# Block-sparse attention and a gated convolution layer on one core: other dummy products and q transposes in the head, a last output block in halves, and a new instruction order

## The chip, the core and the metric

The kernel runs on one core of a Trainium2 chip. The core has a matrix engine (PE), whose weight loads the profile lists apart (PEld), a vector engine (DVE), a scalar engine for activations (ACT), GpSimd (POOL) and a sync engine (SP). Each has its own queue of instructions and takes them in the order in which they were written; they wait for one another by semaphores. PE writes only to PSUM, a small memory of eight banks, from which DVE or ACT copy to the main on-chip memory (SBUF). DMA engines move data between SBUF and the chip's main memory. The metric is the device time of one execution in microseconds, lower is better.

## What is computed

Attention over q, k and v of shape (4, 8, 768, 64) with a mask of 32 x 32 blocks, and behind it a feed-forward layer with a gate made by a convolution over three positions:

```python
scores = (1/8) * q @ k.T                 # per batch and head, 768 x 768
mask   = near blocks | first and last block row and column | 3 drawn blocks a row
attn   = softmax(where(mask, scores, -1e9)) @ v
x      = attn as (4, 768, 512)
h      = relu(x @ w_in)                  # (4, 768, 1024)
c      = conv_w[0]*h[s-1] + conv_w[1]*h[s] + conv_w[2]*h[s+1]
out    = (h * sigmoid(c)) @ w_out        # (4, 768, 512), float32
```

## The kernel before

The kernel first makes a list of operations (`op(...)`): each has a name, the engines on which it may run, a function that writes its instructions, and the buffers that it takes or uses. Then `put_down` writes them in the order of a long string, `ORDER`: two characters choose an operation, a letter (P, A, V, G, S) its engine where it has a choice, and one more character each buffer that it takes. So the string alone sets the order in each engine's queue, the engine of each copy, and the buffer.

**Attention.** The 32 heads are 16 pairs, four to a batch. A sequence of 768 is cut into two segments of 384 positions (the last into 256 and 128), and the work into 144 units, 18 to a segment of 384. A unit is eight blocks of 128 x 128 scores. It has two groups of score products (`s`, L762) into one of two PSUM tiles `st`, one exponential on ACT over 128 x 1024 (`exp`, L773) into a tile `pt`, and two groups of eight products with v (`av`, L795) into `av`. The mask is 24 extra rows of q and k (partitions 64 to 87), so the score product adds it. After a pair's last unit of a segment DVE takes the reciprocal of the sums (`rcp`, L712) and multiplies (`norm`, L714); the result `xtok` is transposed by a DMA or, in four segments, by PE (`x_tr`, L733), with a copy `x_cp`.

**Getting q and k ready.** q and k must lie with the 64 channels on partitions. For pairs 0 to 5 PE transposes them (`k_tr`, L467; `q_tr`, L505 or L535), and DVE or ACT copy from PSUM into the tiles `e` and `o` (`k_cp`, `q_cp`; every such copy has line L341 on DVE and L337 on ACT, the lines of the helper `dcopy`). For later pairs a DMA transposes, and two copies (`stg_cp`) follow. There are two ways to transpose a half of q. `q_head` turns 64 columns at a time, six products for a pair, each giving 64 partitions by 128, and needs two copies, one of two thirds of the columns and one of one third. `q_half` turns 128 columns at a time, so three products for a pair, with two column groups on top of each other in the result, and needs four copies (two of 64 x 256, two of 64 x 128). Before, `q_head` is called for pair 0 alone, once for each head; `q_half` for all others (L548 to L553).

**The start.** Pair 0 is loaded as float32 by SP and ACT queues (k, q, the drawn blocks, then v as SP's fourth large transfer) and cast on chip (`cast_k`, `cast_q`, `v_cp`); pairs 1 to 3 come through POOL's queue, which converts. The mask rows of q come from six small products (`w24`, L311), cast by `m_q` (L321 on ACT, L323 on DVE); those of k by `m_k`. PE runs dummy products on a tile of zeros (`warm` with 256 columns and `fill` with 128, L229 to L233); the first thirteen stand ahead of everything, the others where the order puts them.

**Feed-forward.** For a segment, `f1` (L888) multiplies with w_in into a PSUM tile `mix`, `relu` (L908 on ACT, L910 on DVE) writes `hE`. The gate is, for each pair of channel groups, three `mul` (L940), two `add` (L948), a `tanh` (L987), `g1` (L990) and `g2` (L995, writes `gT`); in the last segment PE does the convolution with diagonal weights (`conv`, L959). `out_block` multiplies 128 positions with w_out, eight products of 512 columns (`f2`, L822), copies out of PSUM (`ev`) and sends 128 x 512 by SP (`out`, L833). In the last segment the sums lie in the tiles `st` (`tail`), which the scores no longer need, and the copy is made in two halves. A batch has six output blocks, t = 0 to 5. At the very end these are left: t = 2 and 3, whose gates come from the last segment but one, and t = 4 and 5 of the last segment. Their f2 steps stand in the order so that t = 3, 5, 2 and 4 end in this sequence.

## Time and profile before

| | |
|---|---|
| median of 3 runs | 214.99 us (214.48, 214.99, 215.62) |
| the profiled execution | 214.71 us |
| its span, first to last instruction | 212.7 us |
| busy: PE, DVE, ACT, POOL | 204.0, 187.9, 193.3, 60.7 us |
| exponentials on ACT | 144 of 1.03 us, 140.4 us busy |
| first and last exponential start | 8.5 and 193.2 us |
| bytes read and written | 23.08 and 6.29 MB |

A row of the timeline has the start in us, the length, the engine, line, operation, the tiles written and read with their shapes, and the count of like instructions merged into it; in brackets the idle time of the engine ahead of it and what ended that. Products on PE overlap: a row's length is that of the pipeline, and the rate is seen in the distance of starts. A row by stretches has the window, its length, then the busy time and count of PE, PEld, DVE, ACT and POOL, the granted clock, the share of DMA and GB/s. A row of the groups has line, engine, operation, tiles, shapes, count, busy us and mean ns of one, then the idle time just ahead.

### The profile page before, as it was taken

To read this page: it belongs to the slowest core of one execution; us is meant where nothing else is said; L and a number is where in the kernel's file an instruction comes from. 1 tells how busy PE (TensorE), PEld (TensorE's weight loads), DVE (VectorE), ACT (ScalarE), POOL (GpSimd) and SP (SyncE) were. 2 spreads that over 40 slices of the span, in tenths; PEclk is the share of its full clock that TensorE was granted. 3 is DMA by queue.
4 is the path that set the end of the run, shared out by engine and by line. 5 is a ranking of instruction groups with operands and counts; after the bars stand their busy time and mean duration, and the time that the engine had idled before them with its cause. 6 is when DMAs were issued, how large, how long until landed. Compare 5 with 4: busy or idle time off the path is not lost.

```text
span 212.7 us, 6843 instructions
## 1 busy us (share of the span) xinstructions
PE 204.0 (96%) x2705; PEld 155.0 (73%) x2705; DVE 187.9 (88%) x595; ACT 193.3 (91%) x258; POOL 60.7 (29%) x117
## 2 busy tenths in 40 slices
PE   7999999999999999999999999999999999999992
PEld 4688877878767776677678867776668867787740
DVE  4779999999998997799999994999999967999970
ACT  6699999799999999999999998999999977998752
POOL 8794145620736143210406153910000000000000
PEclk9999999999999999999999999999999999999999
DMA  6999986799494999894759957996524040010405
GB/s 168 191 172 192 173 112 93 91 160 108 65 128 65 148 194 151 112 139 98 149 97 210 147 81 113 135 134 136 143 84 127 12 127 2 3 54 0 148 3 197
DMA packets 48935, 24.81 MB, mean 117 GB/s; under 512 B 35120, under 2 KB 45832, under 8 KB 48904
## 3 DMA queue, kind: packets, MB, share of 16 engines
q0 software_dynamic: 19728, 11.05, 43.6%
q1 hardware_dynamic: 28888, 13.05, 28.9%
q8 instruction: 21, 0.34, 0.7%
q10 hardware_dynamic: 288, 0.30, 0.4%
q14 instruction: 10, 0.08, 0.1%
HBM read 23.08 MB, written 6.29 MB: 138 GB/s over the span
## 4 chain that ended last, share of the span: by engine, by line
PE 73%; DVE 20%; ACT 2%; DMA 1%; issue 1%; DVEq 0%; ACTq 0%
PE st L762 23%; PE mix L822 18%; PE mix L888 16%; PE av L795 12%; DVE m L940 4%; DVE o L341 4%; DVE e L341 3%; DVE m L948 2%; PE st L822 2%; DVE diag L388 2%; DVE hE L910 2%; DVE xtok L714 2%; DMA o2s<-in_k_dram 1%; ACT pt L773 1%; DVE xT L341 1%
## 5 line engine op out<-in xcount | busy, mean ns | idle before, releaser
L773 ACT ACTIVATE pt<-st 128x1024 bf16<-128x1024 f32 x144 | 140.4, 1029 | 4.5 <-PE st L762 3.7
L795 PE MATMUL av<-vt,pt 128*128 128x65 bf16 x1152 | 59.9, 193 | 0.4 <-DVE xtok L714 0.4
L795 PEld LDWEIGHTS <-pt 128*128 128x128 bf16 x1152 | 52.2, 97 | 9.5 <-ACT pt L773 0.7
L888 PE MATMUL mix<-xT,winb 128*128 128x384 bf16 (+2 forms) x288 | 54.3, 308 | 1.2 <-DVE hE L910 0.8
L940 DVE TENSOR_SCALAR m<-hE,cw 128x382 bf16<-128x382 bf16 (+2 forms) x192 | 49.2, 318 | 0.3
L822 PE MATMUL mix<-woutb,gT 128*128 128x512 bf16 x176 | 47.1, 379 | 0.0
L762 PE MATMUL st<-o 88*128 88x128 bf16 (+1 forms) x240 | 45.1, 230 | 0.0
L762 PE MATMUL st<-o,e 88*128 88x128 bf16 (+1 forms) x228 | 44.0, 235 | 0.3 <-ACT pt L773 0.2
L762 PE MATMUL st<-e,o 88*128 88x128 bf16 (+1 forms) x224 | 43.5, 236 | 0.2
L762 PE MATMUL st<-e 88*128 88x128 bf16 (+1 forms) x208 | 42.3, 243 | 0.6 <-DVE e L341 0.3
L762 PEld LDWEIGHTS <-o 88*128 88x128 bf16 x464 | 35.5, 98 | 8.1 <-issue 0.6
L762 PEld LDWEIGHTS <-e 88*128 88x128 bf16 x436 | 33.6, 98 | 8.7 <-issue 1.7
L948 DVE TENSOR_TENSOR m<-m 128x764 bf16<-128x764 bf16 (+2 forms) x64 | 34.1, 536 | 0.7
L888 PEld LDWEIGHTS <-winb 128*128 128x128 bf16 x288 | 23.5, 97 | 8.7 <-issue 1.8
L987 ACT ACTIVATE m<-m 128x764 bf16<-128x764 bf16 (+2 forms) x32 | 26.2, 823 | 1.7 <-DVE m L948 1.4
L822 PEld LDWEIGHTS <-gT 128*128 128x128 bf16 x192 | 15.7, 97 | 11.8 <-DVE gT L995 1.7
L415 POOL COPY pace<-pt 1x1 bf16<-1x1 bf16 x24 | 8.2, 342 | 55.5 <-ACT pt L773 55.4
L908 ACT ACTIVATE hE<-mix 128x384 bf16<-128x384 f32 (+2 forms) x39 | 18.9, 498 | 1.0 <-PE mix L888 1.0
L995 DVE TENSOR_TENSOR gT<-m,hE 128x764 bf16<-128x764 bf16 (+3 forms) x36 | 18.0, 510 | 0.5
L714 DVE TENSOR_TENSOR xtok<-av,rcp 128x384 bf16<-128x384 f32 (+2 forms) x36 | 18.1, 506 | 0.4
L240 POOL DMA_DIRECT2D nat<-in_q_dram x23 | 16.8, 729 | 2.5 <-issue 2.1
L910 DVE TENSOR_SCALAR hE<-mix 128x384 bf16<-128x384 f32 x25 | 13.7, 553 | 3.1 <-PE mix L888 1.6
(92 smaller groups left out, 174.5 us busy)
## 6 DMA issues: line engine op xcount, KB each, us to landing
out_dram<-o2s SPq DMA_DIRECT2D x24, 256.0 KB, 2.8
nat<-in_k_dram POOLq DMA_DIRECT2D x15, 192.0 KB, 4.7
vn<-in_v_dram POOLq DMA_DIRECT2D x15, 192.0 KB, 5.1
nat<-in_q_dram POOLq DMA_DIRECT2D x6, 192.0 KB, 4.6
winb<-in_moe_w_in_dram POOLq DMA_DIRECT2D x2, 512.0 KB, 8.0
woutb<-in_moe_w_out_dram POOLq DMA_DIRECT2D x4, 256.0 KB, 7.4
nat<-in_q_dram POOLq DMA_DIRECT2D x9, 96.0 KB, 4.7
nq<-in_q_dram POOLq DMA_DIRECT2D x6, 96.0 KB, 3.9
```

The source lines that it names most:

```text
L714: nm = op("norm", {"DVE": t_dps(128 * C)}, lambda e: nc.vector.tensor_tensor(out=xtok_t[xk.index][:, 0:C].rearrange("p c h d -> p h c d"), ...
L762: nc.tensor.matmul(out=st[:, 128 * x:128 * (x + n_)], lhsT=QK[kc % 2][s][0:88, 1, hh, kc // 2, :], rhs=QK[par][s][0:88, 0, hh, idx:idx + n ...
L773: nc.scalar.activation(out=pt_t[ptb.index], in_=st_t[stb.index], func=AF.Exp, bias=0.0, scale=0.125)
L795: nc.tensor.matmul(out=o[:, off:off + 65], lhsT=pt_t[ptb.index][:, 128 * x:128 * x + 128], rhs=V_t[vslot_b[P].index][:, hh, kc, 0:65], sta ...
L822: nc.tensor.matmul(out=acc(), lhsT=gT_t[gb.index][:, ffc, 128 * t:128 * t + 128], rhs=woutb[:, ffc, :], start=(ffc == 0), stop=(ffc == NFF ...
L888: nc.tensor.matmul(out=mix_t[hb.index][:, w1 * y:w1 * y + w1], lhsT=winb[:, fc, 128 * ffc:128 * ffc + 128], rhs=xT_t[xt_buf[n].index][:, f ...
L908: nc.scalar.activation(out=dst, in_=src, func=AF.Relu, bias=0.0, scale=0.5)
L910: nc.vector.tensor_scalar(out=dst, in0=src, scalar1=0.5, scalar2=0.0, op0=ALU.mult, op1=ALU.max)
L940: nc.vector.tensor_scalar(out=m_t[cb.index][:, x, y, 0:w], in0=hE_t[heb.index][:, f0 + y, t0 + x:t0 + x + w], scalar1=cw[:, x, f0 + y:f0 + ...
L948: nc.vector.tensor_tensor(out=m[:, a_, :, 0:w], in0=m[:, a_, :, 0:w], in1=m[:, b_, :, 0:w], op=ALU.add)
L987: th = [op("tanh", {"ACT": t_act(2 * w) + 0.04}, lambda e, cb=cb, w=w: nc.scalar.activation(out=m_t[cb.index][:, 0, :, 0:w], in_=m_t[cb.in ...
L995: nc.vector.tensor_tensor(out=gT_t[gtb.index][:, f0:f0 + 2, t0:t1], in0=m_t[cb.index][:, 0, :, 0:w], in1=hE_t[heb.index][:, f0:f0 + 2, 1 + ...
```

## The change

Four things change.

- The dummy products: 13 of 256 columns and 26 of 128, where there were 14 and 14.
- For pairs 1 to 3 the first half of q goes through `q_head`, both heads in one call: six turns of 64 columns and two copies, of 64 x 512 and 64 x 256, for three turns of 128 columns and four copies. Pairs 4 and 5, and the second halves of all, stay with `q_half`.
- The output block t = 5 of the last batch is made as two column halves. Each has its own bank, eight products of 256 columns, one copy and one DMA of 128 KB. All other output blocks, those of the last segment too, have one copy of 512 columns and one DMA.
- The order string is another one: 1809 operations for 1800. By the engine's letters, ACT has 259 operations before and 254 after, DVE 475 and 473, PE 876 and 891, SP 77 and 78, POOL 113 in both.

The start of the new order, read op by op. PE: 13 wide and 4 narrow dummies, K transposes of head 0, the six mask products, q of head 0, K of head 1, eleven narrow dummies, `cw_t`, the first unit's scores, eight narrow dummies, q of head 1, the second unit's scores, K of pair 1, the third unit's scores, q of pair 1, the fourth unit's. Before, the wide dummies are followed by K of head 0, one dummy, the mask products, q of head 0, six dummies, K of head 1, the first scores, `cw_t`, two dummies, q of head 1, and so on, with eight narrow dummies later. ACT: one mask copy of k, K cast, q cast, both mask casts, two q copies of head 0, the v cast of pair 0, the first exponential, two q copies of head 1, the second exponential. Before: both mask copies of k, the K cast between them, two K copies of head 0, one mask cast, a q copy, a q cast, a K copy of head 1, the first exponential, a q copy, the second, a K copy of pair 1, the third. All K copies are on DVE in the new order, the v cast is not. At the end PE's last steps are: t = 5's first half, its second half, then t = 4, t = 2 and t = 3, the last; the copies are on ACT for the first half of t = 5, for t = 2 and t = 3, and on DVE for the second half and for t = 4. POOL's queue has a few of its first loads exchanged: the second half of pair 1's q stands ahead of pair 2's K, pair 4's K ahead of pair 2's v, and the first half of w_in ahead of pair 4's q.

```diff
-    NWARM, NFILL = 14, 14
+    NWARM, NFILL = 13, 26
...
+        elif P < NF:
+            q_head(0, lambda: nat_t[nb.index][:, 0, 0:384].rearrange("p (h c) -> p h c", h=2), ld_q, nb, due - 3)
         else:
             q_half(0, lambda: nat_t[nb.index][:, 0, 0:384], ld_q, nb, due - 3)
...
-    def out_block(b, t, due, deps, after, tail=False):
-        gb, ob, mb = gt_buf[b], Buf(P_os), Buf(P_tail if tail else P_mix)
...
-        halves = ((0, 256), (256, 512)) if tail else ((0, 512),)
+    def out_block(b, t, due, deps, after, tail=False, last=False):
+        gb, ob = gt_buf[b], Buf(P_os)
+        halves = ((0, 256), (256, 512)) if last else ((0, 512),)
+        outs = []
         for x, (c0, c1) in enumerate(halves):
...
+            mb = Buf(P_tail if tail else P_mix)
...
+                        nc.tensor.matmul(out=acc(), lhsT=gT_t[gb.index][:, ffc, 128 * t:128 * t + 128],
+                                         rhs=woutb[:, ffc, c0:c1], start=(ffc == 0), stop=(ffc == NFFC - 1),
+                                         skip_group_check=True)
...
+            outs.append(op("out", {"SP": 0.6}, lambda e, c0=c0, c1=c1: nc.sync.dma_start(
+                out=out[b, 128 * t:128 * t + 128, c0:c1], in_=o2s_t[ob.index][:, c0:c1]),
+                due + 3, [evo], uses=[ob], dma=("hw", 0.65 if not last else 0.4)))
...
-            out_block(b, t, base + W * 0.75 + 0.12 * W * (t - tok // 128), d, [] if lastn else rl_all, lastn)
+            out_block(b, t, base + W * 0.75 + 0.12 * W * (t - tok // 128), d, [] if lastn else rl_all, lastn,
+                      lastn and t == 5)
```

More of the change, by code (lines that the diff above doesn't have):

```diff
@@ new lines @@
+5P15X5Y6416g06h606165666922rV25R1u1p6i36l16m2u06a6q06r6n46s52x12vV32wV2yV2zV6v16w6b5S06j06A06B2516k6o6x06C16J1
+6K1d6c16d5TV06p6t6u6y27V1q6L26O06P1206z6T16U6D2HV36Q36V41t6E16M6Y06Z6F226V6N6R6S6G6W131s28V751766+56e06X7707a0
+6/707b7c16fV29V710726H0780797f11k1c73174A7g7h27k07l6IV7m3iG0iD1iHiE7p1iFA01r1o2ZV4iIVi/0j07q7r47d7y0iJ07zj22l1
+iK7e7i7j7D17E7A5j12pV7n7I07o2oV2nV7s7u12mV7JiLAiM0iN2/5g1A5h3e15i2A15j3g25k3h3i07F07K17N17v7O2K17t17W07XiOVj3
+7P22LV42MViV07B7C7GiWj71j8iXVj47Y37/17w17xV15l3m25m3o1807H7L7M7Q840814858657R2N08918a8b02B17Z07+j52QV7S2ja2CV
@@ L62 @@
+rXrCrDAry1r4qVrdrzqWrH1rIr5r1r2rAArJ2rY0r6rKrZrp0rj1r+rLr7rM1rkrNrR0rerO0rPrQr8qwrqrSrT2rfrUrgrVqCpsr9rhrapyri
+r/0s51sb2s6s0scs7s8sdses9A3sfVs1sgsas2s3V0s4rlrmrnA2rorrrsrtA1ru
 """
```

105 lines of the change are left out of this document (47 added, 58 removed).

## The prediction

> **What bounds the kernel now.** I read the page's first lines and its chain of work that ended last, then the busy times by stretches, then the timeline of the first 16 us and of the last 8 us.
>
> ```profile
> span 212.7 us, 6843 instructions
> PE 73%; DVE 20%; ACT 2%; DMA 1%; issue 1%; DVEq 0%; ACTq 0%
> 0.00:10.00 10.00, 8.45 (x51) 5.60 (x52) 5.76 (x31) 6.62 (x12) 8.06 (x18) 1.00 0.95 179
> 10.00:20.00 10.00, 9.55 (x147) 8.70 (x146) 8.62 (x27) 9.40 (x11) 7.71 (x13) 1.00 1.26 179
> 20.00:60.00 40.00, 38.45 (x624) 32.16 (x622) 38.76 (x131) 38.25 (x47) 16.56 (x34) 1.00 0.92 119
> 80.00:190.00 110.00, 109.83 (x1453) 82.39 (x1451) 99.91 (x289) 105.44 (x138) 20.91 (x40) 1.00 0.67 109
> 190.00:213.00 23.00, 18.61 (x181) 11.48 (x178) 16.17 (x65) 14.13 (x29) 0.00 (x0) 1.00 0.22 81
> ```
>
> The last five rows give, after the length, the busy time of PE, weight loads, DVE, ACT and POOL. Three stages follow. From 80 to 190 us PE has no gap (109.83 of 110), while DVE has 10 us to spare and ACT 4.6: only less PE work, or an earlier start of it, helps there. From 20 to 60 all three are nearly full, DVE most (38.76 of 40), and PE can be kept waiting. In the first 10 us no compute engine is full: ACT works 6.62, DVE 5.76, and PE's time is partly dummies. The profiled execution took 214.71 us, 2.0 more than its span; the median shown is 214.99. My sum is made against 214.71. The faster and slower below mean more than 0.5% (1.07 us), about what a measurement of this kernel can tell from no change.
>
> **The head.** Each unit is two groups of score products and one exponential. The engines take their instructions in the written order, so the row in front of each exponential says what held it.
>
> ```profile
> 6.38 0.47 ACT L321 CAST o<-st 24x384 bf16<-24x384 f32 x1 [0.41 <-DVE e L323]
> 6.87 0.26 ACT L337 COPY o<-mix 64x128 bf16<-64x128 bf16 x1
> 7.33 0.47 ACT L337 COPY e<-av 64x384 bf16<-64x384 bf16 x1
> 8.54 1.02 ACT L773 ACTIVATE pt<-st 128x1024 bf16<-128x1024 f32 x1 [0.75 <-PE st L762]
> 10.53 1.02 ACT L773 ACTIVATE pt<-st 128x1024 bf16<-128x1024 f32 x1 [0.33 <-PE st L762]
> 11.75 0.80 ACT L337 COPY o<-mix 64x768 bf16<-64x768 bf16 x1 [0.20 <-DVE e L341]
> 12.57 10.34 ACT L773 ACTIVATE pt<-st 128x1024 bf16<-128x1024 f32 x11
> 5.79 0.55 DVE L323 CAST e<-st 24x384 bf16<-24x384 f32 x1 [0.57 <-PE st L311]
> 7.16 0.28 DVE L341 COPY e<-mix 64x256 bf16<-64x256 bf16 x1 [0.82 <-ACT o L337]
> 8.99 0.73 DVE L341 CAST vt<-m 128x768 bf16<-128x768 f32 x1
> 7.50 0.37 PE L762 MATMUL st<-e 88*128 88x256 bf16 x1 [0.21 <-DVE vt L368]
> 11.89 0.31 PE L762 MATMUL st<-o,e 88*128 88x128 bf16 x1
> 12.50 0.22 PE L762 MATMUL st<-o,e 88*128 88x128 bf16 x1
> 8.67 0.39 PE L231 MATMUL av<-warm 128*128 128x128 bf16 x2
> ```
>
> The exponentials start at 8.54, 10.53 and 12.57; from there eleven run without a gap, 10.34/11 = 0.94 us apart. So the third one's start is what the head hands on. It came late because ACT stopped for a 0.80 us K copy at 11.75. PE is at half speed until about 12.4: the same 128-column product takes 0.31 us at 11.89 and 0.22 at 12.50. Starts before that lie 0.107 us apart (two dummies in 0.39, of which one alone is 0.28).
>
> Now the new order, walked with these durations. The mask's first casts both go to ACT: 5.79 + 0.47 + 0.47 = 6.73. The two q copies of head 0 follow there: 64x256 between the 128-wide 0.26 and the 384-wide 0.47, I take 0.37, then 0.26: 7.36. The first scores start at 7.43 (before 7.50) and end at about 8.47; that is no gain yet. Behind the q copies ACT now does the first v cast, before the first exponential. On DVE it took 0.73; the only such copy on ACT is this row:
>
> ```profile
> L337 ACT COPY vt<-vn 128x768 bf16<-128x768 bf16 x1 | 0.8, 832 | 0.0
> m<-in_v_dram SPq DMA_DIRECT2D x1, 384.0 KB
> o2s<-in_k_dram SPq DMA_DIRECT2D x1, 192.0 KB, 3.0
> ```
>
> It waits for v's transfer, issued at 2.06 (SP's fourth). The trace shows no landing. Not before 2.06 + 3.0 = 5.1 (the half as large k load took 3.0) and not after 8.99, where DVE read it without idling. I take 8.2, near the late end, since POOL's loads share the DMA engines. Then: cast to 9.03, first exponential to 10.05, two q copies of head 1 (0.26 + 0.37) to 10.7, second exponential, third at 10.7 + 0.94 = 11.65 if its scores are there. The K copy is gone from ACT (DVE has it). With v at 7.36 or earlier the second exponential stays near 10.5 and the third comes at 11.45; with v at 8.99 it is 12.4. On PE, at half speed: eight dummies behind the first scores, 8.3 + 8 x 0.107 = 9.16, hidden behind the first exponential; q transposes 0.32, eight score blocks 0.85, six K transposes 0.64, eight more blocks 0.85: 11.82, and with 0.18 of latency 12.0. So the third exponential starts between 11.65 and 12.0, or 0.57 to 0.92 earlier. Behind it stand the copies of pair 1 on DVE (two K copies of 0.55, two q copies) with the fifth exponential due at 13.5 to 13.8, against 12.57 + 2 x 0.94 = 14.4. I take **-0.7**, bounds 0 and -1.1.
>
> The dummies themselves: 13 instead of 14 of 256 columns, 26 instead of 14 of 128: 12 x 0.107 - 0.213 = 1.07 us of PE. Eleven of the added ones stand in front of the first scores, where PE waited for ACT and DVE anyway, eight behind them; three are later, at 0.06 each. Cost nothing as long as ACT sets the pace; without that cover the eight cost 0.86.
>
> **q in 64-column turns.** For pairs 1 to 3 six transposes (64 columns of weights, 128 moved) replace three, and two copies replace four.
>
> ```profile
> L505 PE MATMUL mix<-ident,nat 128*64 128x128 bf16 x3 | 0.5, 314 | 0.0
> L341 DVE COPY o<-mix 64x256 bf16<-64x256 bf16 x12 | 3.4, 286 | 1.0 <-ACT e L337 0.4 <-PE mix L535 0.4
> L341 DVE COPY o<-mix 64x128 bf16<-64x128 bf16 x9 | 2.0, 220 | 0.6 <-PE mix L535 0.4
> L341 DVE COPY e<-mix 64x768 bf16<-64x768 bf16 x5 | 2.7, 546 | 0.2 <-PE mix L467 0.2
> ```
>
> PE: nine more turns at 0.107 cold or about half of that warm, 0.5 to 1.0 us, before 25 us, where PE waits; hidden. DVE: before 2 x 0.286 + 2 x 0.220 = 1.01 a pair; after 0.286 and one of 512 columns, which no row shows: between 0.286 and 0.546, on the line between them 0.42. That is 0.3 less a pair, 0.9 in all (bounds 0.5 and 1.3).
>
> By the Trainium skill, "TensorE: Matmul & The Clock Gate", section on the PE-mode transpose, transposes don't count as PE activity for the clock, which speaks against having twice as many. Here the clock came up at about 12.4 although some twelve transposes stood in the 3.4 us before; by that rule exponential three would be at 12.0, by the row at 11.65.
>
> **The new order between.** I counted both order strings, op by op. ACT through the last exponential: four K copies, four relu and one q copy fewer, one mask copy changed for a cast; more: the v cast, two x copies, three output copies; about 1.4 us less. DVE through the gate products at 60 us: four K copies more (1.6 to 1.8, but in 5 to 12 us, where it idles), one mask copy more, six q copies (partly the wider ones), a mask cast, a v copy and an x copy fewer; the sum is 0.1 us less. Through the ninth gate product of the next part (99 us) DVE has 2.4 more: three multiply ops of 0.49, one add of 0.50, two relu of 0.50, the K copies. PE work in front of the 42nd unit's scores is equal within 0.2. Where PE is full this is worth nothing by itself, and what the head gained is passed on. I take -0.1, bounds -1.0 and +1.5.
>
> ```profile
> L910 DVE TENSOR_SCALAR hE<-mix 128x384 bf16<-128x384 f32 x25 | 13.7, 553 | 3.1 <-PE mix L888 1.6 <-ACT pt L773 1.4
> L948 DVE TENSOR_TENSOR m<-m 128x764 bf16<-128x764 bf16 x32 | 17.4, 551 | 0.3
> L940 DVE TENSOR_SCALAR m<-hE,cw 128x382 bf16<-128x382 bf16 x96 | 25.2, 325 | 0.1
> ```
>
> **The tail.**
>
> ```profile
> 204.92 0.64 DVE L995 TENSOR_TENSOR gT<-m,hE 128x512 bf16<-128x512 bf16 x2
> 205.40 2.06 PEld L822 LDWEIGHTS <-gT 128*128 128x128 bf16 x11 [0.43 <-DVE gT L995]
> 206.09 0.59 ACT L337 COPY o2s<-mix 128x512 f32<-128x512 f32 x1 [1.67 <-PE mix L822]
> 207.79 1.02 PE L822 MATMUL st<-woutb,gT 128*128 128x512 bf16 x4
> 208.91 0.42 DVE L341 COPY o2s<-st 128x256 f32<-128x256 f32 x1 [1.57 <-PE st L822]
> 209.36 0.37 ACT L337 COPY o2s<-st 128x256 f32<-128x256 f32 x1 [1.01 <-DVE o2s L341]
> 206.70 3.40 SPq L833 DMA_DIRECT2D out_dram<-o2s  x4
> ```
>
> Today the block t = 4 ends last: its products end at 208.81, then DVE and ACT copy its halves one after the other (208.91 to 209.73, 0.82), then SP issues (206.70 + 3.40 = 210.10 is the end of that issue), and the rest to 212.7 is the transfer. In the new order the block that is split, t = 5, is not the one that ends last: its halves end early, and the last products are the four of t = 3, in one 512-column bank that ACT copies in 0.59: 0.82 - 0.59 = 0.23 less. The transfer is as large as today's last one. What is split (16 products of 256 columns for 8 of 512, one DMA more on SP, 0.33) lies 2.6 us in front of the end: nothing. PE's idle 0.43 at 205.40, waiting for a gate product, may partly go, since the new order puts products that need older gates behind the newest; I take 0.17 of it. Tail **-0.4**; bounds -1.0 (all gaps gone) and +0.4 (a second such wait).
>
> **Sum.** 214.71 - 0.7 + 0.0 (dummies, turns) - 0.1 - 0.4 = 213.5. The profiled execution lies 0.3 under the median of the runs shown, so for a median 213.5 to 213.8; I give **213.6**.
>
> **The rivals.** (1) *The head gain is lost in the stretch where DVE sets the pace.* For it: DVE is busy 38.76 of 40 from 20 to 60, and its work up to 60 us is nearly the same; against it: ACT hands on earlier units and the K copies use idle time. Then only the tail is left: 214.71 - 0.4 = 214.3. (2) *Slower: DVE becomes the bound from 60 to 100 us.* The new order puts 2.4 us more DVE work in front of the gate product at 99 us, and PE takes its output products in written order, so it would stand behind it. It decides once DVE has under 2.4 us of idle time in 60 to 100 less the head's 0.7; against it, the windows show some 10 us of DVE idle time in 80 to 190. Time: 214.71 + 2.4 - 0.4 = 216.7, or 216.5 with a little of the head kept. (3) *The clock comes up a window earlier.* With PE filled from 5.7 on, full speed may come at about 9 instead of 12.4. Then PE's list above ends at 10.9, pair 1's copies move too, the head is worth 1.1 and the copies of pair 1 another 0.5: 214.71 - 1.6 - 0.5 = 212.6. For it, the gaps of 0.2 to 0.4 us in PE before 9 us are what the dummies fill; against it, ACT's own list, 11.65, is the floor. The Trainium skill, "TensorE: Matmul & The Clock Gate", section on the HAM clock gate, gives a free-running window of about 3.4 us that must be busy; 12.4 less 3.4 is 9.0, about where PE's gaps end before.
>
> **Chances.** Forecast 0.46, rival (1) 0.23, (2) 0.18, (3) 0.13. The faster bound is 213.92: of the forecast 0.36 lies under it and 0.10 above, so faster 0.36 + 0.13 = 0.49, same 0.10 + 0.22 = 0.32, slower 0.19 with the rest of (1). The range goes from 212.3 (rival 3 with a full tail) to 216.0, which leaves out most of (2); the forecast's own range is 212.9 to 214.4.
>
> **What would show it.**
>
> ```profile
> L773 ACT ACTIVATE pt<-st x144: 1005/1024/1080, 8.5 to 193.2; 128x1024 bf16<-128x1024 f32 x144
> ```
>
> The third exponential at 11.6 to 12.0 and no K copy before it; the v cast on ACT before the first one, and what ended ACT's idle time there; the start of the first 0.22 us score product; PE without gaps from 80 to 190 and shifted by the head's gain (the last of the 144 exponentials some 0.7 before 193.2); DVE idle time in 60 to 100; the last output copy on ACT alone, 0.59. I am wrong if the first exponential waits for v past 10 us, if the gain of the head is gone by 60 us, or if PE shows DVE waits of over 1 us between 45 and 190.

## The result and the profile after

| | before | changed kernel |
|---|---|---|
| median of 20 runs each | 215.07 us (214.24 to 216.44) | 213.38 us (211.09 to 215.44) |
| the profiled execution | 214.71 us | 214.73 us |
| a repeat of the changed kernel (9 runs) | | 213.22 us (211.28 to 214.37), profiled execution 213.47 |

The changed kernel is faster: the ratio of the times is 0.9904, 95% interval 0.9881 to 0.9926. This ratio leaves out two executions of the changed kernel that lie over 1.5% above its fastest; the ratio of the two medians in the table is 0.992. Its times spread over 4.3 us, where those of the kernel before spread over 2.2. Its profiled execution fell near the slow end of its spread, so stretches are compared below with the repeat's profile, which lies near its median; the head is the same in both.

Two lines of the page of the changed kernel, whose span is 212.7 us: the clock that PE was granted, in 40 slices of the span (9 is full speed), and the chain of work that ended last:

```profile
PEclk9769999999999999999999999999999999999999
...
PE 71%; DVE 10%; DMA 7%; ACT 6%; issue 3%; POOL 1%; SPq 0%; POOLq 0%
```

The shares of the chain moved: DVE's fell from 20% to 10%; transfers, which had 1%, have 7%. And the clock has a dent in the second and third slice, which the kernel before did not have.

The head of the changed kernel, timeline of PE and of ACT (start, length, instruction, idle time ahead and what ended it):

```profile
6.00 0.78 PE L231 MATMUL av<-warm 128*128 128x128 bf16 x11
7.84 0.27 PE L378 MATMUL mix<-ident,cw 24*128 24x24 f32 x1 [1.06 <-DVE e L341]
8.04 0.39 PE L764 MATMUL st<-e 88*128 88x256 bf16 x1
...
7.89 0.83 ACT L337 CAST vt<-m 128x768 bf16<-128x768 f32 x1 [0.66 <-DMA m<-in_v_dram]
9.11 1.02 ACT L775 ACTIVATE pt<-st 128x1024 bf16<-128x1024 f32 x1 [0.38 <-PE st L764]
11.39 1.02 ACT L775 ACTIVATE pt<-st 128x1024 bf16<-128x1024 f32 x1 [0.44 <-PE st L764]
12.88 1.02 ACT L775 ACTIVATE pt<-st 128x1024 bf16<-128x1024 f32 x1 [0.47 <-PE st L764]
14.63 3.89 ACT L775 ACTIVATE pt<-st 128x1024 bf16<-128x1024 f32 x4 [0.72 <-PE st L764]
```

PE stands idle for 1.06 us in front of the transpose of the conv weights (`cw_t`), and the first scores follow it, at 8.04 instead of 7.50. From then on every exponential waits for scores: the third starts at 12.88 (before 12.57), the fourth at 14.63. The eleven dummies at 6.00 run at full speed (0.78 us for 11; in the kernel before, two at 8.67 took 0.39). The 256-column scores at 8.04 take 0.39, as at half speed.

The last copies on ACT of the changed kernel:

```profile
208.32 0.58 ACT L337 COPY o2s<-mix 128x512 f32<-128x512 f32 x1 [1.97 <-PE mix L829]
209.19 0.58 ACT L337 COPY o2s<-mix 128x512 f32<-128x512 f32 x1 [0.28 <-PE mix L829]
```

As forecast, one copy by ACT alone ends the kernel.

Where the time went, as starts of exponentials in the traces (the first is number 0, the last 143):

| stretch | before | repeat of the changed kernel | difference |
|---|---|---|---|
| start to exponential 4 | 14.40 | 15.63 | +1.23 |
| 4 to 24 | 20.36 | 20.39 | +0.03 |
| 24 to 30 | 7.94 | 6.29 | -1.65 |
| 30 to 48 | 19.89 | 20.14 | +0.25 |
| 48 to 60 | 15.71 | 14.83 | -0.88 |
| 60 to 143 | 114.92 | 115.01 | +0.09 |
| 143 to the end of the span | 19.53 | 19.11 | -0.42 |
| span | 212.75 | 211.40 | -1.35 |

So in these two profiles the head lost 1.2 us, the stretch between won 2.2, the tail 0.4. The other versions below with the whole new order have 1.5 to 2.2 less than the kernel before between exponentials 4 and 143; the first profile of the changed kernel, with a wait for a load at 65 us, has 0.9 less.

The row from 24 to 30 overstates its part, because PE does not do the same work in it: it runs 123 instructions there in the order before and 109 in the new one, and between exponentials 30 and 34 it runs 60 and 84. From 24 to 34 the difference is 12.31 - 11.25 = 1.06 us. PE's idle time in that stretch was 0.66 + 0.27 = 0.93 us before and is 0.00 in the repeat.

What filled the stretch between is seen on PE. Busy time by stretches (window, length, then PE, PEld, DVE, ACT, POOL), first before, then the repeat:

```profile
20.00:30.00 10.00, 9.41 (x180) 8.51 (x178) 9.55 (x37) 9.67 (x12) 3.50 (x8) 1.00 0.96 146
30.00:40.00 10.00, 9.45 (x143) 7.70 (x141) 9.73 (x34) 9.51 (x12) 4.80 (x10) 1.00 0.74 102
40.00:60.00 20.00, 19.58 (x308) 15.95 (x306) 19.48 (x62) 19.08 (x24) 8.26 (x17) 1.00 0.99 114
60.00:80.00 20.00, 19.15 (x266) 14.66 (x263) 18.63 (x58) 19.45 (x27) 7.47 (x14) 1.00 0.97 134
```

```profile
20.00:30.00 10.00, 10.00 (x187) 9.09 (x188) 9.27 (x36) 9.78 (x11) 4.07 (x10) 1.00 0.98 143
30.00:40.00 10.00, 9.98 (x143) 8.06 (x142) 9.45 (x35) 9.98 (x14) 4.12 (x9) 1.00 0.77 107
40.00:60.00 20.00, 19.88 (x318) 16.42 (x316) 19.39 (x63) 19.89 (x24) 9.68 (x15) 1.00 0.75 101
60.00:80.00 20.00, 19.96 (x284) 15.57 (x283) 19.45 (x61) 19.72 (x26) 8.20 (x14) 1.00 1.29 151
```

PE's gaps from 20 to 80 us were 0.59 + 0.55 + 0.42 + 0.85 = 2.41 us and are 0.00 + 0.02 + 0.12 + 0.04 = 0.18. The sums of the waits of PE in that window (engine, line waited for, us, times, longest) name them; before, then the repeat:

```profile
PE mix L888 <- DVE hE L910: 0.6, 1, 0.6
PE mix L467 <- DVE o L341: 0.5, 1, 0.5
PE av L795 <- DVE xtok L714: 0.4, 1, 0.4
PE st L762 <- ACT pt L773: 0.2, 1, 0.2
PE mix L888 <- DVE e L341: 0.2, 1, 0.2
```

```profile
PE st L764 <- DVE e L341: 0.2, 1, 0.2
```

The windows lie at the same times of both spans, so the units in them are not quite the same. Four of the five waits were for DVE. DVE has no less to do now: from 20 to 80 us it was busy for 9.55 + 9.73 + 19.48 + 18.63 = 57.39 us and is for 9.27 + 9.45 + 19.39 + 19.45 = 57.56. Its work stands in another order.

### The profile page after: what moved, and what is told of

It is laid out like the page before. It is cut to its first block, busy times and chain, and to the rows that moved or that the text cites. A ratio compares the mean times of both kernels' runs of the same rounds, so it can differ in the third digit from the quotient of the medians.

```text
span 212.7 us, 6879 instructions
## 1 busy us (share of the span) xinstructions
PE 203.4 (96%) x2713; PEld 157.3 (74%) x2733; DVE 188.7 (89%) x593; ACT 191.7 (90%) x253; POOL 62.3 (29%) x117
## 3 DMA queue, kind: packets, MB, share of 16 engines
HBM read 23.08 MB, written 6.29 MB: 138 GB/s over the span
## 4 chain that ended last, share of the span: by engine, by line
PE 71%; DVE 10%; DMA 7%; ACT 6%; issue 3%; POOL 1%; SPq 0%; POOLq 0%
PE st L764 25%; PE mix L894 16%; PE mix L829 14%; PE av L797 12%; ACT pt L775 4%; DVE m L946 3%; DMA nq<-in_q_dram 3%; DMA nat<-in_k_dram 2%; DMA o2s<-in_q_dram 2%; DVE m L954 2%; DVE gT L1001 2%; DVE m L996 1%; DVE o L341 1%; DVE e L341 1%; PE mix L467 1%
## 5 line engine op out<-in xcount | busy, mean ns | idle before, releaser
L829 PE MATMUL mix<-woutb,gT 128*128 128x512 bf16 x156 | 44.5, 379 | 1.2 <-DVE gT L1001 0.3
L764 PE MATMUL st<-o 88*128 88x128 bf16 (+1 forms) x240 | 44.3, 231 | 0.1
L764 PE MATMUL st<-e,o 88*128 88x128 bf16 (+1 forms) x224 | 42.9, 237 | 0.1
L764 PEld LDWEIGHTS <-o 88*128 88x128 bf16 x464 | 34.8, 98 | 6.4 <-issue 0.5
L415 POOL COPY pace<-pt 1x1 bf16<-1x1 bf16 x24 | 8.9, 373 | 55.5 <-ACT pt L775 55.2
L829 PEld LDWEIGHTS <-gT 128*128 128x128 bf16 x200 | 16.5, 97 | 9.8 <-DVE gT L1001 0.8
L914 ACT ACTIVATE hE<-mix 128x384 bf16<-128x384 f32 (+2 forms) x35 | 17.2, 507 | 0.7 <-PE mix L894 0.6
L916 DVE TENSOR_SCALAR hE<-mix 128x384 bf16<-128x384 f32 x29 | 15.9, 556 | 1.9 <-PE mix L894 1.3
```

Of the source, the lines that this page charges most:

```text
L764: nc.tensor.matmul(out=st[:, 128 * x:128 * (x + n_)], lhsT=QK[kc % 2][s][0:88, 1, hh, kc // 2, :], rhs=QK[par][s][0:88, 0, hh, idx:idx + n ...
L829: nc.tensor.matmul(out=acc(), lhsT=gT_t[gb.index][:, ffc, 128 * t:128 * t + 128], rhs=woutb[:, ffc, c0:c1], start=(ffc == 0), stop=(ffc == ...
L914: nc.scalar.activation(out=dst, in_=src, func=AF.Relu, bias=0.0, scale=0.5)
```

## The experiments

Each of the versions below is the changed kernel with one edit, unless said otherwise. The kernel before, measured beside them, had a median of 215.15 us beside the first four, 214.71 beside the two with a cut, the last block in the shared tile and the v cast, and 214.66 beside the other four. A ratio is to the kernel before measured beside that version. Edits that lie in the order string are shown by the names of the operations. Line numbers in the rows differ by one or two between versions.

**The changed kernel again.** No edit.

> The changed kernel as it is, for a second profile and as the yardstick of the three kernels beside it. Theory (the head hands on an earlier start, and the matrix engine's clock in the first 15 us decides how much): about 213.4 us, 1.6 to 2.0 under the kernel before; a profile whose clock does not fall back after its first rise has its third exponential at 11.6 to 12.0 us and a time near 212.3, one whose clock falls back has it at 12.5 to 13 and a time near 214. Rival (the gain comes from the order further on and the tail): the time does not go with the clock of the head.

Median 213.22 us (9 runs, 211.28 to 214.37), ratio 0.9903 (0.9869 to 0.9938). This is the yardstick for the rest.

**The conv weights' transpose behind the first scores.** PE's order:

```diff
-k_tr1, fill4-fill14, cw_t0, s0, s1, fill15-fill22
+k_tr1, fill4-fill14, s0, s1, cw_t0, fill15-fill22
```

> One edit: the transpose of the convolution weights (cw_t) stands behind the first scores instead of in front of them. Theory (in the changed kernel PE stood 1.06 us in front of it, for the 12 KB transfer that is queued behind v on SP, and the first scores and the clock suffered): the first scores start at 7.3 instead of 8.0, PE's idle time there falls to 0.5 or less, 0.5 to 1.0 us faster than the changed kernel, 212.5 to 212.9. Rival (the first exponential waits for the v cast on ACT, which ended at 8.72, so PE's wait is covered): within 0.3 us of the changed kernel.

Median 211.62 us (6 runs, 210.97 to 213.31), ratio 0.9851 (0.9811 to 0.9891). Its PE and ACT rows:

```profile
7.47 0.42 PE L765 MATMUL st<-e 88*128 88x256 bf16 x1
...
8.46 0.30 PE L379 MATMUL mix<-ident,cw 24*128 24x24 f32 x1
...
8.72 1.02 ACT L776 ACTIVATE pt<-st 128x1024 bf16<-128x1024 f32 x1
...
10.43 3.78 ACT L776 ACTIVATE pt<-st 128x1024 bf16<-128x1024 f32 x4
```

The first scores start at 7.47, the walk's 7.43 within 0.04, and from 10.43 four exponentials run without a gap: the third starts at 11.35, the fifth at 13.19, 2.44 earlier than in the repeat. At the end of the span 1.82 of that is left (209.58 for 211.40). In the medians the place of one transpose of 0.3 us is worth 1.6 us here, more than the 0.5 to 1.0 that was expected. This is not the transpose alone: the clock took another course in this profile. It rose once, at 9.26, and stayed; in the repeat it rose at 4.20, fell at 7.62 and came back at 14.44. The two are told apart further down.

**The dummies of the kernel before.**

```diff
-    NWARM, NFILL = 13, 26
+    NWARM, NFILL = 14, 14
```

with the 28 dummies at the places that they had in the order before.

> The changed kernel with the dummy products of the kernel before, 14 wide and 14 narrow, at the places that they had there. Theory (the dummies act by the clock, which comes up earlier with more of them): full speed comes first at 11 to 15 us, the third exponential at 12 to 12.6, 0.5 to 1.0 us slower than the changed kernel, about 214.2. Rival (the dummies cost as much as they bring, or the clock falls back anyway): within 0.3 us, or up to 0.5 faster.

213.39 us (9 runs, 212.42 to 214.58), ratio 0.9925 (0.9900 to 0.9949): no change that can be told from 213.22, where 0.5 to 1.0 us slower was expected. The clock did rise as late as expected, at 12.72, and the third exponential came at 12.15; but the repeat with its early rise was no quicker, since its clock fell back. With the transpose in front of the scores, the new dummies brought nothing that the medians show.

**q by halves again for pairs 1 to 3.**

```diff
-        elif P < NF:
-            q_head(0, lambda: nat_t[nb.index][:, 0, 0:384].rearrange("p (h c) -> p h c", h=2), ld_q, nb, due - 3)
         else:
             q_half(0, lambda: nat_t[nb.index][:, 0, 0:384], ld_q, nb, due - 3)
```

> The changed kernel with the first halves of q of pairs 1 to 3 made as before, three turns of 128 columns and four copies each, at the same places of the order. Theory (the turns of 64 columns save DVE 0.3 us a pair where DVE sets the pace): 0.3 to 0.9 us slower than the changed kernel. Rival (ACT sets the pace there and DVE has room; PE saves nine turns): within 0.3 us, or faster by up to 0.5.

213.27 us (6 runs, 212.78 to 213.95), ratio 0.9914 (0.9886 to 0.9943): no change in the median either. The comparison is not a clean one: the clock rose once, at 13.40, in this profile, and all six runs have a mean clock of 0.998 or more, against four of the repeat's nine. The stretch from 24 to 30 takes 6.29 us here too, so it doesn't come from the turns. The wide copy was sized rightly. The row of the groups of the repeat up to 30 us:

```profile
L341 DVE COPY e<-mix 64x512 bf16<-64x512 bf16 x3 | 1.2, 410 | 0.0
```

0.41 us, where 0.42 was estimated. That DVE's saving is worth nothing because PE and the clock set the pace there is an explanation that no run tests by itself.

**Old order up to a cut, new order behind it.** Two kernels run the order of the kernel before (its dummies and q turns too) through exponential 20, or through 34, and then the new order and the new tail.

```diff
+ORDER = before's operations through exp 20 (or 34), then the changed kernel's
```

> The order of the kernel before through the 21st exponential (with its dummies and its turns of 128 columns), from there the order of the changed kernel, tail included. Theory (the head of the changed order costs some 1.2 us by the fifth exponential, and the gain comes from the stretch between the 25th and the 31st exponential, which took 7.94 us before and 6.29 after, plus 0.5 behind it and 0.4 in the tail): 212.0 to 212.6, faster than the changed kernel, with 6.3 to 6.6 us from the 25th to the 31st exponential. Rival (the changed head is what makes the later order run well, by what it moves to DVE early): the stretch stays near 7.9 and the time at 213.5 to 214.2.

> The same with the cut behind the 35th exponential: the order before through the stretch in question, then the changed one. Theory: the stretch from the 25th to the 31st exponential stays at 7.9 us, only the 0.5 of the body and the 0.4 of the tail are left: 213.8 to 214.3. Rival (the order further on carries the gain): 212.0 to 213.2.

Cut at 20: 213.45 us (12 runs), ratio 0.9949 (0.9929 to 0.9969). Cut at 34: 213.54 us (12 runs), ratio 0.9954 (0.9927 to 0.9981). With the head as before, the order behind exponential 34 and the tail are worth some 1.2 us. The theory that the stretch from 24 to 30 carries the gain would have put the two over 1 us apart; 0.09 us lies within their spread, so the times don't bear it out. The profiles show why. ACT's rows around exponentials 27 to 30, cut at 20, then cut at 34:

```profile
39.53 3.76 ACT L773 ACTIVATE pt<-st 128x1024 bf16<-128x1024 f32 x4
```

```profile
39.38 3.05 ACT L773 ACTIVATE pt<-st 128x1024 bf16<-128x1024 f32 x3 [0.36 <-PE st L762]
42.80 0.26 ACT L337 COPY e<-mix 64x128 bf16<-64x128 bf16 x1 [0.37 <-DVE o L341]
```

Cut at 34 keeps two gaps of the kernel before (0.36 and 0.37), cut at 20 has four exponentials in a row. From exponential 24 to 30 it is 7.64 us against 6.28. But most of the difference is work that stands elsewhere: from exponential 20, up to which the two orders are the same, to 34, behind which they are the same again, it is 16.75 us cut at 34 and 16.66 cut at 20. On the way the version cut at 20 takes 5.37 us for 4.75 from 20 to 24 and 5.01 for 4.36 from 30 to 34. So with the old head the new order in this stretch saves 0.09 us, as the medians say. What it saves with the new head is not shown by a run of its own. Behind exponential 34, the version cut at 34 has 0.78 us less than the kernel before up to the last exponential (145.37 for 146.15) and 0.43 less in the tail; that is the 1.2 of its medians.

**The last block whole.** Block t = 5 in one bank with one copy; first in the bank beside that of t = 4, in the same PSUM tile `st`, then in the other tile.

```diff
             out_block(b, t, base + W * 0.75 + 0.12 * W * (t - tok // 128), d, [] if lastn else rl_all, lastn,
-                      lastn and t == 5)
+                      False)
```

> The changed kernel with the last output block t = 5 whole: eight products of 512 columns, one copy on ACT, one DMA; its place in the order kept. Theory (the block that ends last is t = 3, so the halves of t = 5 lie in front of the end and the tail's gain comes from the order alone): within 0.2 us of the changed kernel, 19.1 us from the last exponential's start to the end. Rival (the halves free ACT and DVE in time for the last copies): 0.2 to 0.5 slower.

> The changed kernel with its last block (t=5) whole again, as in the whole-block variant before it, but in the other PSUM tile of the two rather than in the one that holds block t=4. Theory (halves are worth nothing; what the whole block cost there, 0.7 us, was its products standing behind the copy of the neighbouring bank of the same tile): the end behind the last exponential's start is 19.1 us again, within 0.2, and the idle 0.72 us of PE in front of the last four products is gone. Rival (the halves themselves save the copy of 512 columns behind the last product): the end stays at 19.4 to 19.8 us.

In the shared tile: 213.07 us (12 runs, 211.84 to 214.68), ratio 0.9934 (0.9906 to 0.9962), not to be told from the repeat; but in the profile the end behind the last exponential is 19.82 us, 0.7 longer, where the theory allowed 0.2. In the other tile: one execution, 211.41 us, and an end of 18.95, 0.16 shorter than with halves. PE's last products, shared tile, then other tile:

```profile
201.95 2.79 PE L829 MATMUL st<-woutb,gT 128*128 128x512 bf16 x12
205.46 1.02 PE L829 MATMUL st<-woutb,gT 128*128 128x512 bf16 x4 [0.72 <-ACT o2s L337]
206.32 1.89 PE L829 MATMUL mix<-woutb,gT 128*128 128x512 bf16 x8
```

```profile
200.39 3.65 PE L829 MATMUL st<-woutb,gT 128*128 128x512 bf16 x16
203.88 1.89 PE L829 MATMUL mix<-woutb,gT 128*128 128x512 bf16 x8
```

In the shared tile the products of one bank wait 0.72 us for ACT's copy out of the other bank. That copy is the one of t = 5, and the four products are the last of t = 4. Without that wait the halves are worth nothing, as forecast. (The 211.41 is of a single execution, in which the clock rose once and stayed. For the tail only its end is read; its head is the changed kernel's and is read below.)

**The v cast on DVE.** With `cw_t` moved as above, and pair 0's v cast on DVE behind its last mask copy.

```diff
-v_cp0 on ACT, in front of exp 0
+v_cp0 on DVE, behind m_slot1
```

> The changed kernel with the transpose of the convolution weights behind the first scores and, besides, the v cast of pair 0 on DVE behind its second slot copy instead of on ACT in front of the first exponential. Theory (in the kernel with the first edit alone the first exponential starts at 8.72, when the v cast ends, and DVE is idle for over 1 us at 10 to 12): first exponential at 8.2 to 8.4, 0.2 to 0.5 us faster than with the first edit alone, 211.1 to 211.4. Rival (the second and third exponential wait for PE and for the q copies anyway): within 0.2 us of it.

Median 211.67 us (7 runs, 210.79 to 213.87), ratio 0.9880 (0.9849 to 0.9910): not to be told from the version with the cast on ACT. Its profiled execution, 213.87, is its slowest run: the first exponential came at 8.54, the second only at 11.46. The clock rose at 4.42 and fell at 7.83 there, although the transpose stands behind the scores: PE waited 0.80 us for ACT's q copy instead, in front of the first scores at 7.59.

**The load of the conv weights ahead of v**, with `cw_t` where the changed kernel has it.

```diff
-    ld_cw = dma("ld_cw", "SP", lambda: cw0, moe_conv_w.rearrange("k (f p) -> (k f) p", p=128), 8, service=0.05, after=[ld_v0])
+    ld_cw = dma("ld_cw", "SP", lambda: cw0, moe_conv_w.rearrange("k (f p) -> (k f) p", p=128), 8, service=0.05)
```

> The changed kernel with one transfer moved: the load of the conv weights (12 KB) is issued on SP ahead of the load of v instead of behind it; their transpose stays in front of the first scores. Theory (PE waited there for this transfer, although the row names a copy on DVE): the transpose starts at 6.7 to 7.0 us instead of 7.84, the first scores at about 7.3 and the first exponential no later than 8.6. Rival (PE waited for DVE's copy of K, as the row says): the transpose stays at 7.5 to 7.9 us and the first scores at 7.7 to 8.1.

One execution, 211.61 us. Its PE rows:

```profile
6.31 1.38 PE L232 MATMUL av<-warm 128*128 128x128 bf16 x11
7.62 0.30 PE L379 MATMUL mix<-ident,cw 24*128 24x24 f32 x1
7.85 0.39 PE L765 MATMUL st<-e 88*128 88x256 bf16 x1
```

The rival's numbers came (transpose at 7.62, scores at 7.85), but not by its cause: the clock was still at half speed, the dummies held PE until 7.6, the transpose followed them without a gap, and DVE's copy of K ended only at 7.75. The load had landed at 5.06. By the time of the transpose alone the run does not tell the two causes apart. The packets of the transfer do. In the traces the conv weights are 24 packets of 512 bytes; in each run in which PE stood idle in front of the transpose:

| version | last packet ends | `cw_t` starts | difference | DVE's copy from `av` into `e` ends |
|---|---|---|---|---|
| changed kernel | 7.22 | 7.84 | 0.62 | 7.85 |
| repeat | 7.39 | 7.91 | 0.52 | 7.86 |
| dummies of before | 7.13 | 7.75 | 0.62 | 7.95 |
| q by halves | 7.38 | 7.89 | 0.51 | 8.46 |
| last block, shared tile | 6.99 | 7.60 | 0.61 | 7.80 |
| transpose moved, v cast on DVE | 8.14 | 8.76 | 0.62 | 8.58 |
| transpose moved, dummies of before | 7.15 | 7.79 | 0.64 | 7.87 |

The distance to the last packet is 0.5 to 0.6 us each time. The DVE copy that the row in the first profile names ends behind the start of the transpose in five of the seven, so it can't be what released it. And in the five versions of the table behind the repeat the profile itself names the transfer. The rows of the last block in the shared tile, which has the changed kernel's head, and of the transpose moved with the dummies of before:

```profile
7.60 0.26 PE L378 MATMUL mix<-ident,cw 24*128 24x24 f32 x1 [0.87 <-DMA cw<-in_moe_conv_w_dram]
...
7.79 0.21 PE L378 MATMUL mix<-ident,cw 24*128 24x24 f32 x1 [0.17 <-DMA cw<-in_moe_conv_w_dram]
```

So it was a load of 12 KB, queued behind v on SP, in front of which PE stood, and behind PE the first scores.

**The transpose moved, all 26 narrow dummies in front of the first scores.**

```diff
-warm12, fill0-fill3, k_tr0, w24, q_tr0, k_tr1, fill4-fill14, s0, s1, cw_t0, fill15-fill22
+warm12, fill0-fill3, k_tr0, fill4-fill6, w24, q_tr0, k_tr1, fill7-fill25, s0, s1, cw_t0
```

> The changed kernel with the conv weights' transpose behind the first scores and all 26 narrow dummies in front of the first scores (4 behind the wide ones, 3 behind head 0's K transposes, 19 behind the next), so that PE has no pause there. Theory (what is left of the spread of the changed kernel is its clock falling back after a first rise): the clock rises once and stays, mean granted clock 0.998 or more in most executions, median 211.0 to 211.5 us. Rival (the dummies run at half speed and only push the first scores back to about 8.0 us; the clock is as before): 211.8 to 212.3 us.

Median 211.27 us (6 runs, 210.98 to 213.87), ratio 0.9866 (0.9821 to 0.9910); in five of the six the mean granted clock is 0.999 or 1.000. These are the numbers that the theory gave.

**The transpose moved, the dummies of the kernel before.**

> The changed kernel with the conv weights' transpose behind the first scores, and with the dummies of the kernel before (14 wide, 14 narrow, at their old places). Theory (the number of dummies matters little; the place of that transpose is what the changed head lost by): 211.6 to 212.2 us, within 0.5 us of the version with the transpose moved alone (211.62). Rival (the moved transpose gained because the longer row of dummies brings the clock up a window earlier): the clock rises only at 12 to 13 us and the median is 212.3 to 212.8 us.

Median 213.04 us (6 runs, 211.53 to 213.45), ratio 0.9906 (0.9872 to 0.9940). The theory failed (211.6 to 212.2): with the dummies of before, moving the transpose is worth 213.39 - 213.04 = 0.35 us in the medians, and the ratios' intervals overlap. The rival's mechanism, a rise only at 12 to 13 us, failed too: the clock rose early, at 5.02, and fell back. Windows of 3.41 us from the first rise of the clock (busy time of PE first, clock behind POOL), of this version, then of the one with all dummies in front, then of the repeat:

```profile
5.02:8.43 3.41, 2.82 (x30) 1.94 (x31) 3.12 (x10) 2.24 (x6) 3.41 (x6) 1.00 1.24 224
8.43:11.85 3.42, 3.42 (x27) 2.71 (x26) 2.95 (x7) 3.25 (x6) 2.13 (x4) 0.50 1.44 194
11.85:15.26 3.41, 3.41 (x40) 3.21 (x39) 2.23 (x6) 1.45 (x3) 3.41 (x6) 0.50 1.34 199
```

```profile
5.19:8.60 3.41, 3.37 (x45) 2.76 (x46) 3.27 (x11) 1.82 (x6) 3.02 (x5) 1.00 1.19 189
8.60:12.02 3.42, 2.40 (x31) 1.86 (x30) 2.79 (x7) 3.42 (x6) 1.68 (x4) 1.00 1.42 191
```

```profile
4.20:7.61 3.41, 2.24 (x29) 1.58 (x26) 3.08 (x12) 1.72 (x5) 3.41 (x5) 1.00 1.10 202
7.61:11.03 3.42, 3.12 (x23) 2.48 (x24) 2.30 (x5) 2.38 (x4) 1.65 (x4) 0.50 1.41 191
11.03:14.44 3.41, 3.41 (x27) 2.77 (x26) 1.72 (x4) 2.05 (x2) 3.26 (x5) 0.50 1.32 191
```

After an early rise the clock stayed where PE was busy for 3.37 of the next 3.41 us, and fell for two windows where it was busy for 2.82 or less. That is one profiled execution against five (the changed kernel, the repeat, the whole block in the shared tile and the v cast on DVE had 2.12 to 2.38), so it is a correlation; that fullness of this one window decides is not proved, for the next window of the second version had only 2.40 and the clock stayed.

**The head by the course of the clock.** The profiles of all versions fall into three courses, and the start of exponential 4 goes with the course, not with the place of the transpose:

| course of the clock in the profile | version: rise, start of exponential 4 |
|---|---|
| rises once, by 10 us, and stays | all dummies in front: 5.19, 13.14; transpose moved: 9.26, 13.19; last block in the other tile: 9.71, 13.41; load ahead of v: 9.87, 13.44 |
| rises once, at 12 to 14 us | before: 12.46, 14.40; cut at 34: 13.26, 14.59; dummies of before: 12.72, 14.66; q by halves: 13.40, 14.83; cut at 20: 13.83, 14.86 |
| rises at 4 to 5 us, falls, rises again at 14 to 15 | transpose moved, dummies of before: 15.00; last block in the shared tile: 15.46; repeat: 15.63; changed kernel: 15.67; transpose moved, v cast on DVE: 15.73 |

The last block in the other tile has the changed kernel's head, transpose in front. Its rows:

```profile
7.59 0.30 PE L378 MATMUL mix<-ident,cw 24*128 24x24 f32 x1
7.90 0.37 PE L764 MATMUL st<-e 88*128 88x256 bf16 x1
...
10.69 3.75 ACT L775 ACTIVATE pt<-st 128x1024 bf16<-128x1024 f32 x4
```

The first scores start at 7.90, 0.43 later than with the transpose moved, and exponential 4 only 0.22 later; the spans are 209.44 (its tail is 0.16 us shorter) and 209.58. The version with the load ahead, transpose in front as well, has 209.59. So where the clock takes the same course, the place of the transpose costs nothing that is left at the end. Its price, as far as the profiles show, is paid by way of the clock. In an early rise the dummies end at 6.8, PE stands until the load has landed, and the clock falls. At half speed the pause is short, but it may cost a window too: with q by halves PE waited 0.18 us for the load, was busy for 3.23 us of the window from 6.58 to 9.99, and the clock rose only at 13.40, while it rose behind the windows with 3.39 to 3.42 us in the three versions that rose at 9.26 to 9.87.

How often an execution was quick can be counted. Executions under 212.2 us: of the changed kernel and its repeat 5 of 29; with the transpose moved 4 of 6; with the v cast on DVE too, 5 of 7; with all dummies in front 5 of 6; with the dummies of before 2 of 6. The mean clock alone doesn't tell the quick ones: it reads 0.984 in each of the five profiles with a fall, but 0.998 to 1.000 in profiles with one late rise too, and the two slow executions with the transpose moved, 213.17 and 213.31 us, have 0.999 and 1.000. No version is a clear best among those with the transpose moved and the new dummies: 211.27, 211.62 and 211.67, with overlapping intervals. The three together have 14 of 19 executions under 212.2; singly, the intervals of their ratios still overlap that of the changed kernel.

## Why the prediction was right, and where it was not

The total was right: 213.6 forecast, 213.38 measured, and faster. Two of its terms were wrong and cancelled, so that the sum came out is luck. Besides, the head has no single price: it depends on the course of the clock, and the median is one of a mixture.

- **The head, -0.7 (bounds 0 and -1.1): wrong, it was +1.23 at the fifth exponential of the repeat.** The step that failed is "the first scores start at 7.43". The walk followed ACT's list and DVE's and took the scores to wait for the q copies alone. It did not walk PE's own list, in which the conv weights' transpose had come to stand in front of the scores, and did not ask when its input lands: SP issues that load behind v, whose landing the walk did estimate. Moving the transpose away brought 7.47. The first exponential still came where the walk had it, at 9.11 and 9.18 for 9.03. What was late was PE's list behind it, which paces the next exponentials as long as PE runs at half speed: the third came at 12.88 and 12.95, where 11.65 to 12.0 was forecast. Where the clock rose at 9.71 with the same head, it came at 11.60.
- **Full speed at about 12.4, as before: wrong in many executions.** The walk counted every product up to the third exponential at 0.107 us and let the exponentials behind it follow at 0.9. In the profile the clock rose at 4.36 and fell at 7.77, and full speed came back only at 14.60, so the fifth exponential came 2.8 us behind the third. At half speed the same instructions fill a window, at full speed they leave part of it empty; in the changed order the 1.06 us of waiting lay in just that window. Of the 29 executions of the changed kernel and its repeat, 12 have a mean clock of 0.985 or less, about what two low windows make. Rival (3), full speed at about 9 us, came true in the profile of the last block in the other tile, which has this head: 9.71, third exponential at 11.60 (the rival's floor was 11.65), and 211.41 us, lower than the rival's 212.6. How many of the 29 took this course is not known; the 11 with a mean clock of 0.998 or more have a median of 212.54 us, but late rises may be among them.
- **v's landing, estimated at 8.2, then the v cast on ACT: right.** The cast waited for the transfer 0.66 us in the changed kernel (7.89) and 1.29 in the repeat (8.32). Putting it on DVE changed nothing that the medians show.
- **Dummies and 64-column turns, 0.0: right as far as the medians tell**, by two versions within 0.2 us of the repeat, whose profiles have another course of the clock. With the transpose moved, the new dummies have 211.62 us and the old ones 213.04, with overlapping intervals of the ratios.
- **The order between, -0.1 (bounds -1.0 and +1.5): wrong in size, -2.16.** The step that failed is the sum of busy times by engine: the new order has the same DVE work up to 60 us, so it was held to be worth nothing. But a sum can't show which instruction stands in front of which. PE's waits for DVE from 20 to 80 us were the price, and the windows that were quoted had it: 38.45 of 40 busy from 20 to 60. In the new order these waits are gone; which of DVE's instructions changed places to that effect was not followed one by one. ACT's rows between exponentials 27 and 30 show one place, of the kernel before, where a gap follows a gap, and of the repeat, where there is none:

```profile
38.72 3.05 ACT L773 ACTIVATE pt<-st 128x1024 bf16<-128x1024 f32 x3 [0.38 <-PE st L762]
42.42 0.26 ACT L337 COPY e<-mix 64x128 bf16<-64x128 bf16 x1 [0.65 <-DVE o L341]
```

```profile
38.85 0.83 ACT L993 ACTIVATE m<-m 128x764 bf16<-128x764 bf16 x1
39.58 3.76 ACT L775 ACTIVATE pt<-st 128x1024 bf16<-128x1024 f32 x4
```

- **Rival (2), slower by DVE from 60 to 100 us: did not come.** PE is busy for 39.88 of the 40 us from 60 to 100 in the repeat, although DVE has only 2.06 us of idle time there, less than the rival asked for. In the profiled execution of the changed kernel another wait stands there, for a load of q on POOL's queue, which the repeat does not have; by exponential 60 the two are 1.11 us apart, most of the 1.26 us by which their times differ. Its row in PE's timeline:

```profile
65.32 0.34 PE L535 MATMUL mix<-ident,nq 128*128 128x128 bf16 x3 [0.78 <-DMA nq<-in_q_dram]
```

- **Rival (1), the head's gain lost in the stretch paced by DVE: could not be seen, as the head had no gain in these profiles.** With the transpose moved it is seen in part: 2.44 us against the repeat at exponential 4, 1.90 at exponential 30, 1.82 at the end.
- **The tail, -0.4: right**, 0.42, and by the step named: the block that is split doesn't end last, and one copy of 0.58 by ACT ends the kernel.

## What to carry to other kernels

When an order changes, walk the list of every engine on the way to the first result, the matrix engine's own list too, and ask of each instruction that has come to the front when its transfer lands. Here a transpose of 0.3 us that needed a 12 KB load made PE stand for 1.06 us, and versions with it further back have medians 1.6 us and more lower, by the profiles mostly because the clock took a better course. Compare the course of the clock in two profiles before giving a difference to anything else. Do not price a reordering by sums of busy time per engine: sum the waits of the engine that should be full, by name, and ask which of them the new order removes. A stretch between two landmarks measures a gain only if the same work lies in it. Where warm-up products are meant to bring the clock up, fill the time up to the first real products without a pause at full speed, not only at half speed; that this keeps the clock up is seen in one profile here and in five of six executions. Judge by the share of executions, not by one profile.

## What the runs showed of the hardware

- After an early rise (4.2 to 5.0 us) the clock fell back after exactly one window of 3.41 us in five profiles and stayed low for 6.83 us, although PE was busy for 3.1 to 3.4 us of the first low window. The longest pause of PE in the window before the fall was 1.06 us in the changed kernel, 1.12 in the repeat and 0.42 in the version with the transpose moved and the dummies of before. The Trainium skill, "TensorE: Matmul & The Clock Gate", section "HAM oscillation — how this bites in real kernels", says that no pause of PE should be longer than about 3.4 us; here much shorter ones went with a fall. The period agrees with the 3413 ns of its section "Part 1: The HAM clock gate (the "warmup" mystery)".
- A window in which PE was busy did not always bring the clock up. With the transpose moved PE was busy for 3.40 of the 3.41 us from 2.43 to 5.84, and the clock rose only at 9.26, behind a window with 3.42; the early rises at 4.20 and 5.02 came behind windows with 3.14 and 3.13. What else decides is not shown.
- The clock column by windows reads 1.00 also ahead of the first rise: before 12.46 us in the kernel before, where a 128-column product took 0.31 us for 0.22 behind it. So a mean clock of 1.000 doesn't exclude a late rise: q by halves has it with a rise at 13.40. The length of a known product tells more than the column.
- A releaser can be named wrongly when a transfer and a copy end close together: the transpose's row in the changed kernel names DVE, and the packets name the load.
- In this program products into one bank of a PSUM tile waited 0.72 us for a copy out of the tile's other bank; into another tile they did not wait.
